# Two halves of the product with v, or one: where twelve matmuls of each head stand in TensorE's queue

## The chip, the cores and the metric

One core of a Trainium2 chip runs the whole program. The metric is device time in microseconds of one execution: 716.66 us before, the median of three runs (716.38 to 716.92). A NeuronCore has five engines, each with an instruction queue of its own that it works through in program order: TensorE (PE in the rows; its weight loads are PEld), VectorE (DVE), ScalarE (ACT), GpSimd (POOL) and SyncE (SP, which issues most DMAs here). They meet by semaphores. TensorE writes to PSUM; VectorE and ScalarE read it.

## The reference

Two layers, one after the other. First, attention over 2 batches x 8 heads of 768 positions and head size 64: q and k are each hashed to a bucket of 6 sign bits (the signs of q @ proj and k @ proj); a score counts only where the buckets agree, all others become -1e9; softmax over a row; product with v. Second, a mixture of 4 experts on the 1536 rows of 512 columns (the 8 heads side by side): for each expert, relu(x @ w1) @ w2, times the expert's normalized share, summed.

```python
mask = q_bucket[:, :, :, None] == k_bucket[:, :, None, :]
scores = np.where(mask, scale * np.matmul(q, k.transpose(0, 1, 3, 2)), -1000000000.0)
attn = np.exp(scores - np.max(scores, axis=-1, keepdims=True))
attn = attn / (np.sum(attn, axis=-1, keepdims=True) + 1e-09)
x = np.matmul(attn, v)                    # heads side by side: 1536 x 512
for e in range(E):
    out += p[:, e:e + 1] * (np.maximum(x @ w1[e], 0.0) @ w2[e])
```

## The kernel before

Everything is unrolled, and the order in the program is the order on each engine. First batch 0's attention runs alone (to about 131 us); then the experts for batch 0 run on TensorE with batch 1's attention interleaved; then the experts for batch 1.

Attention is written out as a software pipeline. A head has 768 query rows, six tiles of 128, and one tile is begun per step; `seq` lists the 96 tiles, step i begins tile i, and head x owns steps 6x to 6x+5 (called steps 0 to 5 of that head below). In each step, operations are issued in the order of the string `ORDER = "TXSUVMEYNRP"`, each for the tile or head that is due after its lag:

- **T** (`stage_t`, batch 0 only; lag 3): six 128x128 transposes on TensorE (L477) of a tile of exponentials into two PSUM banks (`ptps`), and two copies out of them, the first by ScalarE (L483), the second by VectorE (L481) in two of three steps and by ScalarE in the third. The copies go to `pt` (first three tiles of a head) or `pth` (last three).
- **S** (`stage_s`, lag 0): four matmuls (L409, L411) make the tile's scores in one of two PSUM buffers (`sps`); the hash bits are in the stacked operands, so that a wrong bucket falls away. VectorE copies them to `p` with a row reduction (L416), which frees the buffer.
- **U** (`stage_u`): when a head's product with v is finished, ScalarE (L560) copies its first half of rows out of PSUM and VectorE (L558) the second, into `xf`. `xf` holds a pair of heads (even and odd) and has one buffer per half.
- **V** (`stage_v`): the product with v. For each of six 128-row chunks of keys, two matmuls stand side by side in the array (`tile_position`), one per half of the head's query rows: twelve matmuls, each two records in the trace, accumulating in one PSUM bank `pv`. V is issued in parts.
- **M** (`stage_m`, lags 10 and 11, only after odd heads): GpSimd divides the pair by the row sums and splits it into two operands for the experts (L571, L573, L576), one half of the rows per step.
- **E** (`stage_e`, lag 1): ScalarE's exponential with the row sum (L432; an accumulator read follows it).
- **N**, **R**: reciprocal of the row sums on VectorE (L443, L444), and DMAs that turn and spread it.
- **P**: preparation of the next head. In step 1 ScalarE makes the high part `ah` (L338) and GpSimd copies it; in step 2 VectorE makes the low part `al` (L341); in step 3 four matmuls on TensorE make the hash (`hps`, L353), ScalarE takes its signs (`k`, L363), and GpSimd makes the bits (L368, L232); in step 5 VectorE turns the head after it (`xt`, L299). For the heads of batch 1 from the second on, the hash and high part stand in step 0.
- **X**, **Y**: batch 1's transposes by VectorE (L496) and DMA, in place of T.

Between steps, from the middle of batch 0, a generator adds the splits of the first expert's weights: VectorE's high parts (`w1hi`, `w2hi`, L705) and GpSimd's low parts (L698).

A lag counts from the head's last tile: lag 4 of a head is step 3 of the next head, lag 6 its step 5, lag 7 step 0 of the head after, lag 9 step 2. The banks `ptps`, `hps`, `pv` (and later the experts' `mps`) share four PSUM buffers. The lags of V are picked by batch, and U's lag follows from V's last one (`LAG_U` is 3 for batch 0); the last head of batch 0 has `LAST_V = (4, 5)`:

```python
def v_lags(b, h):
    return LAST_V if (b, h) == (0, H - 1) else LAG_V[not mixed(b, h)]
def u_lag(b, h):
    return v_lags(b, h)[-1] + (1 if (b, h) == (0, H - 1) else LAG_U[not mixed(b, h)])
```

`mixed` is true for the eight heads of batch 0.

Of the kernel before, what the change touches and what calls it, by code (L numbers as in the profile page):

```python
# [25 lines left out]
LAG_T = 3  # L26
LAG_X = 2
LAG_Y = 4
LAG_V = ((4, 6), (7,))
LAST_V = (4, 5)  # L30
LAG_U = (3, 1)
LAG_M = (10, 10)
# [19 lines left out]
def tile_lsh_attention__then__domain_moe(  # L52
# [345 lines left out]
    def mixed(b, h):  # L398
        return b * H + h < LIGHT_FROM
# [186 lines left out]
    def v_lags(b, h):  # L586
        return LAST_V if (b, h) == (0, H - 1) else LAG_V[not mixed(b, h)]

# [491 lines left out]
```

## Time and profile before

| | |
|---|---|
| median of three runs | 716.66 us |
| profiled execution | 716.44 us |
| its span | 714.7 us (the rest, 1.74 us, lies around it) |
| TensorE busy | 704.7 us, 99% of the span |
| VectorE / ScalarE / GpSimd busy | 482.1 / 293.3 / 302.6 us |
| granted TensorE clock | 1.00 |
| first batch's attention | from the start to about 131 us |

A busy share is an average over all stages: in the first 131 us VectorE and ScalarE have far more to do than later. Matmul records overlap (one begins while the one before drains), so what a group of matmuls costs is read from one group's start to the start of the next, not from its length. The same holds on ScalarE and VectorE, where the next instruction begins some 0.1 us before the last one's record ends. A bracket at the end of a row gives the idle time of that engine before the row, and what ended it.

### The profile page before, as it was taken

What the parts mean: (1) busy time and instruction counts of PE and PEld (TensorE: products, weight loads), DVE (VectorE), ACT (ScalarE), POOL (GpSimd) and SP (SyncE); (2) the same over time, 40 slices, a digit from 0 to 9 for tenths busy, and PEclk for the clock granted to TensorE, in tenths of its full rate; (3) what the DMA queues carried; (4) which work ended last, traced back from release to release, by engine and by line L of the source; (5) the groups of instructions that cost most, each with busy time, mean ns of one, the idle gap of its engine ahead of it and who ended that gap; (6) DMA issues with size and microseconds to landing.
All of it is one profiled execution on the core that took longest, in us unless ns stands there. A gap on an engine that the chain in (4) does not pass through costs nothing.

```text
span 714.7 us, 10131 instructions
## 1 busy us (share of the span) xinstructions
PE 704.7 (99%) x3750; PEld 597.3 (84%) x3750; DVE 482.1 (67%) x802; ACT 293.3 (41%) x580; POOL 302.6 (42%) x283
## 2 busy tenths in 40 slices
PE   8999999999999999999999999999999999999997
PEld 6766675787977979798888889898998989989896
DVE  6898898875756658575633234986858667685863
ACT  6887888442423324413120103443524434353340
POOL 6359578513255335240422244743424234342420
PEclk9999999999999999999999999999999999999999
DMA  6323344777867977777765112331122022121202
GB/s 148 65 49 76 73 98 92 210 180 191 249 155 209 239 209 188 214 207 240 231 203 137 59 46 74 89 119 59 60 89 88 30 89 59 60 79 69 89 1 88
DMA packets 90848, 87.76 MB, mean 123 GB/s; under 512 B 53168, under 2 KB 55728, under 8 KB 90800
## 3 DMA queue, kind: packets, MB, share of 16 engines
q1 hardware_dynamic: 89776, 86.80, 44.4%
q8 instruction: 29, 0.48, 0.3%
q10 hardware_dynamic: 1024, 0.33, 0.2%
q14 instruction: 19, 0.16, 0.1%
HBM read 65.04 MB, written 22.07 MB: 122 GB/s over the span
## 4 chain that ended last, share of the span: by engine, by line
PE 92%; DVE 3%; ACT 2%; POOL 1%; issue 1%; DMA 0%; POOLq 0%; DVEq 0%; ACTq 0%
PE mps L737 12%; PE mps L739 12%; PE mps L738 12%; PE pv L531 8%; PE mps L797 6%; PE mps L798 6%; PE mps L799 6%; PE sps L411 4%; PE sps L409 4%; PE ptps L477 4%; PE mps L952 2%; PE mps L948 2%; PE mps L951 2%; PE pd L948 2%; PE pa L952 2%; PE pa L951 2%
## 5 line engine op out<-in xcount | busy, mean ns | idle before, releaser
L737 PE MATMUL mps<-w2hi,hh 128*128 128x512 f32 (+1 forms) x388 | 151.1, 389 | 0.0
L739 PE MATMUL mps<-w2hi,hl 128*128 128x512 f32 (+1 forms) x388 | 150.7, 388 | 0.0
L738 PE MATMUL mps<-w2lo,hh 128*128 128x512 f32 (+1 forms) x388 | 150.5, 388 | 0.0
L731 DVE SCALAR_TENSOR_TENSOR acc<-mps,pe,acc 128x512 f32<-128x512 f32 (+1 forms) x85 | 63.0, 741 | 69.5 <-PE mps L739 69.0
L432 ACT ACTIVATE p<-p,nb 128x768 f32<-128x768 f32 x96 | 89.5, 932 | 34.7 <-DVE p L416 34.2
L416 DVE TENSOR_SCALAR_CACHE_REDUCE p<-sps 128x768 f32<-128x768 f32 x96 | 90.0, 939 | 18.8 <-PE sps L411 17.5
L803 ACT ACTIVATE hh<-mps 128x384 fp32r<-128x384 f32 x64 | 31.4, 491 | 170.0 <-PE mps L799 170.0
L934 POOL TENSOR_TENSOR w2lo<-ws,w2hi 128x512 fp32r<-128x512 f32 x32 | 40.6, 1288 | 108.4 <-ACT w2hi L933 108.4
L797 PE MATMUL mps<-xs,w1hi 128*128 128x384 f32 x256 | 86.3, 337 | 0.0
L798 PE MATMUL mps<-xs,w1hi 128*128 128x384 f32 x256 | 86.1, 336 | 0.1
L799 PE MATMUL mps<-xs,w1lo 128*128 128x384 f32 x256 | 86.0, 336 | 0.0
L739 PEld LDWEIGHTS mps<-w2hi,hl 128*128 128x128 f32 x388 | 72.9, 188 | 15.5
L737 PEld LDWEIGHTS mps<-w2hi,hh 128*128 128x128 f32 x388 | 72.9, 188 | 15.0 <-issue 1.2
L738 PEld LDWEIGHTS mps<-w2lo,hh 128*128 128x128 f32 x388 | 73.0, 188 | 14.1
L698 POOL TENSOR_TENSOR w1lo<-ws,w1hi 128x512 fp32r<-128x512 f32 x32 | 41.3, 1292 | 93.4 <-DVE w1hi L705 66.9
L804 DVE SCALAR_TENSOR_TENSOR hl<-mps,hh 128x384 fp32r<-128x384 f32 x64 | 35.6, 557 | 63.6 <-ACT hh L803 63.0
L531 PE MATMUL pv<-pt,tv 128*64 128x384 f32 x288 | 67.1, 492 | 0.0
L698 POOL TENSOR_TENSOR w2lo<-ws,w2hi 128x512 fp32r<-128x512 f32 x32 | 41.3, 1291 | 56.1 <-DVE w2hi L705 41.5
L409 PE MATMUL sps<-ah,q 128*128 128x384 f32 x192 | 53.9, 362 | 1.2 <-DVE p L416 1.2
L893 POOL TENSOR_TENSOR w1lo<-ws,w1hi 128x512 fp32r<-128x512 f32 x24 | 37.0, 1546 | 36.4 <-ACT w1hi L889 23.1
L531 PEld LDWEIGHTS pv<-pt,tv 128*64 128x64 f32 x288 | 24.9, 136 | 32.0 <-issue 31.1
L411 PE MATMUL sps<-k,al 76*128 76x384 f32 x192 | 49.9, 340 | 1.0 <-POOL k L232 0.6
(137 smaller groups left out, 1386.3 us busy)
## 6 DMA issues: line engine op xcount, KB each, us to landing
ws<-in_moe_w_dram SPq DMA_DIRECT2D x64, 512.0 KB, 4.0
scr<-t SPq DMA_DIRECT2D x16, 1152.0 KB, 8.2
pt<-scr SPq DMA_DIRECT2D x64, 288.0 KB, 5.9
tv<-in_v_dram SPq DMA_DIRECT2D x16, 192.0 KB, 5.0
tqk<-in_q_dram SPq DMA_DIRECT2D x30, 96.0 KB, 3.2
out_dram<-acc SPq DMA_DIRECT2D x11, 256.0 KB, 2.0
tqk<-in_k_dram SPq DMA_DIRECT2D x28, 96.0 KB, 3.5
rdb<-row SPq DMA_DIRECT2D x14, 192.0 KB, 5.1
```

Source lines behind the costliest of these rows:

```text
L409: nc.tensor.matmul(ps[:, i, :NH], q1[:, sl], k1[:, i * NH : (i + 1) * NH], start=True, stop=False)
L411: nc.tensor.matmul(ps[:, i, :NH], q2[0:MQE, sl], k2[0:MQE, i * NH : (i + 1) * NH], start=False, stop=True)
L416: nc.vector.tensor_scalar(out=two(pt), in0=ps[:, :, :NH], scalar1=MASKED, scalar2=MASKED, op0=ALU.min, op1=ALU.min, accum_out=nb,)
L432: nc.scalar.activation(pt, pt, ACTF.Exp, bias=nb, scale=-1.0, accum_out=dens[b, h, r][:, o : o + 1])
L531: nc.tensor.matmul(dst, vvs[b, h][:, c], pts[b, h, g][c], start=c == 0, stop=c == NT - 1, tile_position=(0, g * D),)
L698: nc.gpsimd.tensor_tensor(out=lo[:, c - 1], in0=st[c - 1], in1=hi[:, c - 1].bitcast(F32), op=ALU.subtract)
L737: nc.tensor.matmul(ps, hh[:, ts], w2hi[:, f, cs], start=n == 0, stop=False)
L738: nc.tensor.matmul(ps, hh[:, ts], w2lo[:, f, cs], start=False, stop=False)
L739: nc.tensor.matmul(ps, hl[:, ts], w2hi[:, f, cs], start=False, stop=n == FC - 1)
L797: nc.tensor.matmul(ps[:, :SB], w1hi[:, kk, fs], xhi[b, kk][:, sl], start=kk == 0, stop=False)
L798: nc.tensor.matmul(ps[:, :SB], w1hi[:, kk, fs], xlo[b, kk][:, sl], start=False, stop=False)
L799: nc.tensor.matmul(ps[:, :SB], w1lo[:, kk, fs], xhi[b, kk][:, sl], start=False, stop=kk == KD - 1)
```

## The change

One constant. For heads 0 to 6 of batch 0, V is issued in one part at lag 4 (step 3 of the next head) and no more in two halves at lags 4 and 6 (steps 3 and 5). As `stage_v` divides the six chunks by the number of parts, the one part has all twelve matmuls. As U's lag is counted from V's last, U of these heads moves from lag 9 to lag 7. Head 7 (`LAST_V`) and batch 1 (second entry) are as before.

```diff
-LAG_V = ((4, 6), (7,))
+LAG_V = ((4,), (7,))
```

## Rows read from the trace of the kernel before

**Rows 1.** The page: busy time by engine, and VectorE's costliest attention line.
```profile
PE 704.7 (99%) x3750; PEld 597.3 (84%) x3750; DVE 482.1 (67%) x802; ACT 293.3 (41%) x580; POOL 302.6 (42%) x283
...
L416 DVE TENSOR_SCALAR_CACHE_REDUCE p<-sps 128x768 f32<-128x768 f32 x96 | 90.0, 939 | 18.8 <-PE sps L411 17.5
```

**Rows 2.** Busy time by stretch: start:end, length, engines, clock, DMA share, GB/s.
```profile
24.03:37.60 13.57, 13.57 (x90) 9.53 (x89) 10.64 (x21) 11.35 (x25) 6.00 (x8) 1.00 0.36 63
37.60:51.24 13.64, 13.64 (x90) 9.51 (x89) 12.11 (x27) 11.21 (x25) 6.56 (x9) 1.00 0.33 60
51.24:65.81 14.57, 13.87 (x89) 9.51 (x88) 11.74 (x24) 11.57 (x25) 12.83 (x14) 1.00 0.14 39
65.81:79.40 13.59, 13.59 (x90) 9.54 (x89) 11.11 (x22) 11.23 (x25) 7.27 (x9) 1.00 0.68 154
79.40:93.15 13.75, 13.72 (x89) 9.51 (x88) 12.47 (x24) 11.66 (x25) 12.01 (x13) 1.00 0.10 28
93.15:107.68 14.53, 13.55 (x89) 9.57 (x88) 13.41 (x25) 11.13 (x25) 9.36 (x11) 1.00 0.53 102
107.68:122.05 14.37, 14.17 (x87) 8.91 (x86) 12.01 (x23) 12.27 (x26) 12.47 (x14) 1.00 0.38 73
```

**Rows 3.** Timeline of TensorE over one head: start us, us, instruction.
```profile
37.60 0.54 PE L531 MATMUL pv<-pt,tv 128*64 128x384 f32 x1
...
37.97 0.48 PE L531 MATMUL pv<-pt,tv 128*64 128x384 f32 x1
...
39.58 0.82 PE L353 MATMUL hps<-xt,pf 128*44 128x384 f32 x4
40.33 0.87 PE L477 MATMUL ptps<-ident,p 128*128 128x128 f32 x6
...
41.74 1.05 PE L477 MATMUL ptps<-ident,p 128*128 128x128 f32 x6
...
43.42 0.54 PE L531 MATMUL pv<-pt,tv 128*64 128x384 f32 x1
...
45.51 0.88 PE L477 MATMUL ptps<-ident,p 128*128 128x128 f32 x6
```

**Rows 4.** Timeline of ScalarE over the same head.
```profile
40.51 1.16 ACT L363 ACTIVATE k<-hps,sgn_bias 44x384 fp32r<-44x384 f32 x2 [1.13 <-PE hps L353]
...
42.59 0.94 ACT L432 ACTIVATE p<-p,nb 128x768 f32<-128x768 f32 x1
...
43.90 0.92 ACT L432 ACTIVATE p<-p,nb 128x768 f32<-128x768 f32 x1
...
46.10 0.49 ACT L483 ACTIVATE pth<-ptps 128x384 f32<-128x384 f32 x1 [1.18 <-PE ptps L477]
...
47.45 0.87 ACT L483 ACTIVATE pth<-ptps 128x384 f32<-128x384 f32 x2
48.21 0.94 ACT L432 ACTIVATE p<-p,nb 128x768 f32<-128x768 f32 x1
```

**Rows 5.** Timeline of all engines in a step before the first V.
```profile
15.47 0.94 ACT L432 ACTIVATE p<-p,nb 128x768 f32<-128x768 f32 x1
...
16.55 0.33 PE L477 MATMUL ptps<-ident,p 128*128 128x128 f32 x1 [0.71 <-ACT p L432]
```

**Rows 6.** Timeline of all engines: M's last operations, and U of head 2.
```profile
62.97 1.01 POOL L576 TENSOR_TENSOR xs<-xf,xs 128x384 fp32r<-128x384 f32 x1
...
65.51 0.56 DVE L558 COPY xf<-pv 64x384 f32<-64x384 f32 x1
...
91.03 1.02 POOL L576 TENSOR_TENSOR xs<-xf,xs 128x384 fp32r<-128x384 f32 x1
```

**Rows 7.** Timeline of all engines at the change from batch 0 to batch 1.
```profile
115.35 0.98 DVE L299 STREAM_TRANSPOSE xt<-tqk 128x768 f32<-128x768 f32 x1
...
117.09 0.53 PE L353 MATMUL hps<-xt,pf 128*44 128x384 f32 x2
...
120.36 1.14 DVE L341 SCALAR_TENSOR_TENSOR al<-xt,qk_scale,ah 128x768 fp32r<-128x768 f32 x1
```

## The prediction

> **What bounds the kernel now.** I read the page's busy times first, then busy time by stretch over the first batch, then the timelines of TensorE, ScalarE, VectorE and GpSimd around one head, then what each waits for. The reader should see that TensorE is busy for 704.7 of 714.7 us [rows 1], and that the first batch is a strict rhythm: from one head's V to the next takes 13.57 to 14.57 us [rows 2]. TensorE's busy time fills these stretches to within a hair in four of them and lacks 0.70 and 0.98 us in two, so TensorE's instruction stream sets the pace. But ScalarE is busy for 11.13 to 12.27 us and VectorE for 10.64 to 13.41 us of each [rows 2], both in program order with little room. The granted clock is 1.00 in all of them.
>
> One head's rhythm on TensorE [rows 3]: first part of V at 37.60, hash matmuls (in P) at 39.58, step 4's T and S from 40.33, step 5's from 41.74, second part of V at 43.42, and the next step's T at 45.51. A step without V thus costs 1.41 us, the first part 1.98 and the second 2.09. ScalarE [rows 4] waits exactly twice in this head, each time behind a part of V: 1.13 us for the hash (before the sign at 40.51) and 1.18 us for the transposes after the second part (46.10). Between the two it runs almost without a gap: exponentials start at 42.59 and 43.90, and after 46.10 it runs on through the copies at 47.45 and the exponential at 48.21.
>
> **The change part by part.** *Moved: the second part of V, seven times.* Heads 0 to 6 have LAG_V's first entry; head 7 has LAST_V, batch 1 the second entry. The same 12 matmuls (24 records) are issued; the second six come two steps earlier, between the first six and the hash. Merged they take 1.98 + 6 pairs x 0.32 (39.58 less 37.97, over five) = 3.90 us against 1.98 + 2.09 = 4.07. So 0.17 us a head is saved on TensorE itself, 1.2 us in all [rows 3]. The switches between tile shapes cost this. The Trainium skill (TensorEngine Tiling (Array Packing), Tiling Modes, Key Properties) says that changing the tiling mode drains TensorE; the trace agrees with its 0.17 us, and by that alone the change would be faster (first rival).
>
> *What loses its cover.* Set zero at the start of step 4's T (40.33). On ScalarE the sign starts at +0.18, then come step 4's two copies, the exponential E of step 3's scores at +2.26 and, after one copy, the next at +3.57 [rows 4]. All that follows the hash, so none of it moves against it. T needs an exponential three steps old in scores: in step 0 of the next head T wants the one begun at +2.26. How soon can it follow? An E began at 15.47 and the T that waited for it went at 16.55 [rows 5]: 1.08 us, its accumulator read included. Before, T of step 0 came at 45.51 = +5.18 and E had long ended. Now it could start at +3.09, where V's second part stood, and must wait to 2.26 + 1.08 = 3.34. Going on: ScalarE's copy for step 0 follows E at 3.57 + 0.93 = 4.50. Then U, which the change also moves (below), is taken at 0.37, like a copy of the same width (43.90 less 42.59 less 0.93). The next E starts at 5.24; two copies (48.21 less 47.45, 0.76) and its own 0.93 later the next, at 6.93. TensorE: T of step 1 at 3.34 + 1.41 = 4.75 (its E: 3.57 + 1.08 = 4.65, in time); T of step 2 at 6.32 (E 5.24 + 1.08; TensorE ready at 6.16); T of step 3 at 8.01 (6.93 + 1.08; ready at 7.73). V follows 1.44 later, at 9.45. With 3.90 for V and 0.75 for the hash (40.33 less 39.58) the period is 14.10 us, where a TensorE that waited for nobody would need at most 13.64 - 0.17 = 13.47. The same read from ScalarE: its 11.1 to 11.3 us of work stays, its two waits of 1.13 and 1.18 become one of about 2.9, because after the last E of a head nothing in its queue can run before the sign, and the sign stands behind the whole of V. V's time is what ScalarE and VectorE used to catch up in; split, both halves were used, merged, half is wasted.
>
> *Moved: U, from lag 9 to lag 7.* u_lag is the last lag of V plus 3, so U of heads 0 to 6 comes two steps earlier too, in step 0 where it stood in step 2. No DMA is issued by V or U, so SP's queue is as before, and M (lags 10, 11, on GpSimd) stays. ScalarE's and VectorE's copies (0.37 and 0.48 us from start to start) only change places; the PSUM bank of pv comes free two steps sooner. T of step 3 ran 0.14 us longer than others before, by the timeline for want of a bank, so this is worth between 0 and 0.14 us a head; I take 0, as T of steps 2 and 3 now waits for E anyway.
>
> *A wait that this adds.* The buffer xf has one copy; U of an even head writes it after M of the odd head before has read it. For head 2 M's last GpSimd operation began at 62.97 and took 1.01, and VectorE's U began at 65.51 [rows 6]: 1.5 us of room, and U is moved up by two steps, some 2.8 us. M's place is fixed to V by the chain VectorE al, GpSimd ah, w1lo, M, al, k, M: its end was 63.98 - 51.24 = 12.74 after V; with U out of step 2 al starts about 0.1 us sooner, so 12.64, which is +7.99 after step 4's T (V and hash take 4.65). VectorE would be ready for U at +6.4 to +6.9. VectorE's U takes 0.48 from start to start. Queued behind it: the reduction of step 1's scores (0.94 to 0.95 us [rows 1]), which releases the score buffer that S of step 3 needs (two buffers). So U 8.04 to 8.52, reduction to 9.47, S of step 3 at 9.52 and not at 8.59, V at 10.39: the period from V of head 2 to V of head 3 is 15.04. Likewise at head 4: M ended at 92.05, 12.65 after V at 79.40, less 0.2; U 7.85, reduction to 9.28, period 14.85. At head 6 M (its chain ends 11.3 after V) is early enough. Bounds of this wait: 0, if GpSimd runs ahead, and 1.6 us (7.99 less 6.4) a time.
>
> *The sum, interval by interval against [rows 2].* Head 0 to 1: 14.10 - 13.57 = +0.53. 1 to 2: 14.10 - 13.64 = +0.46. 2 to 3: 15.04 - 14.57 = +0.47; the 0.70 us that TensorE lost there (14.57 less 13.87, nearly all for GpSimd's k by the waits) stays but now runs while ScalarE catches up. 3 to 4: 14.10 - 13.59 = +0.51. 4 to 5: 14.85 - 13.75 = +1.10. 5 to 6: the old loss of 0.98 us (T behind a VectorE copy that stood behind w2hi) goes, as that T now comes 2 us later; but a row's reciprocal and the turn of the next head on VectorE make the reduction of step 0 end near 7.5, so 14.67 - 14.53 = +0.14. After head 6's V: in step 0 of batch 1's first head a second hash (117.09) needs the turned tile xt, made from 115.35 to 116.33 [rows 7]. V's second part stood before it as cover; now TensorE waits there some 1.2 us (xt ready at +5.9, TensorE at +4.7). VectorE's al (120.36, +9.95) comes at about +9.15, zero comes 1.92 later after V than before, and U's 0.48 has gone from VectorE's chain behind it, which ends the batch: 1.92 - 0.80 - 0.48 = +0.64. Sum: +3.85 us. From there TensorE is full, so the delay passes to the end. The profiled execution took 716.44, so 720.3; the median of the runs is 0.22 higher, so 720.5.
>
> **The rivals.** *Faster: TensorE alone decides.* If the exponentials turn out to be ready (ScalarE 82% busy, so it could be), only the switches count: 7 x 0.17 = 1.2 us, with the sooner free PSUM bank up to 7 x 0.31 = 2.2: 714.5 to 715.5. The point from which it decides is E's 1.08 us: T of step 0 must find its E done by +3.09, 0.25 us sooner than I have it, and T of step 3 by 7.6. For it: TensorE's full stretches [rows 2]; against it: ScalarE's gapless runs [rows 4] and T's wait in the steps before the first V [rows 5]. The rule of the Trainium skill to look at the most-contended engine by occupancy (Perfetto Trace Analysis, Identifying the Most-Contended Engine) stands on this side: TensorE's work only shrinks. 10%.
>
> *No change.* ScalarE's waits come out at half my size and the xf wait at zero: 5 x 0.25 + 0.3 - 1.2, so 717.0. 17%.
>
> *Only ScalarE's hole, no wait on xf.* Then head 2 to 3 is 14.10 (-0.47), 4 to 5 is 14.10 (+0.35): 3.85 - 0.94 - 0.75 = +2.2, 718.8. 20%.
>
> *VectorE becomes the bound in each head.* It has 12.1 to 13.4 us of work in three intervals; if each costs the 1.10 of head 4 to 5: 6 x 1.1 + 0.64 = +7.2, 723.9. Against it: its own hole behind V swallows al and the weight casts. 8%.
>
> **How the numbers follow.** The forecast has 45%. Slower by over 0.2% (1.4 us, about what can be told from no change here) are it, the hole alone and the last rival, 0.73 less 0.01 for the hole's lower edge: 0.72; within 0.2%: 0.18; faster: 0.10. The range from 716.8 to 722.5 leaves out the faster rival, half of no change and the last.
>
> **What would show it.** Right: 24 records of V in a row for 3.90 us; ScalarE waiting about 2.9 us before the sign and no more 1.18 after V; T of steps 0, 2 and 3 put down to E; VectorE's U of heads 2 and 4 waiting for GpSimd's last M; the hash of batch 1's first head waiting for xt; intervals near 14.1. Wrong: intervals near 13.4, T not waiting for E, or a first batch that ends on time while the loss comes later.

## The result, and the profile after

The changed kernel takes 722.68 us (median of four runs, 722.4 to 723.07) against 716.79 before (four runs): +5.9 us, a ratio of 1.0086 with a 95% interval of 1.0073 to 1.0098. Slower was forecast, at 720.5 with 722.5 as the range's upper end; the measured time lies 0.2 us above that end.

The page after: busy time by engine, and the line that answers to the second of [rows 1].

```profile
PE 706.7 (98%) x3750; PEld 599.3 (83%) x3750; DVE 479.8 (67%) x802; ACT 292.6 (41%) x580; POOL 303.3 (42%) x283
...
L416 DVE TENSOR_SCALAR_CACHE_REDUCE p<-sps 128x768 f32<-128x768 f32 x96 | 89.9, 938 | 30.8 <-PE sps L411 30.1
```

No engine has more instructions than before [rows 1]: VectorE's 802 take 2.3 us less of busy time, TensorE's 3750 are busy for 2.0 us more. What has grown is VectorE's idle time ahead of its reductions, 18.8 to 30.8 us, put down to scores from TensorE that come late.

Busy time by stretch, from one head's V to the next, answering to [rows 2] (same columns):

```profile
24.79:38.87 14.08, 13.82 (x90) 9.47 (x89) 10.83 (x22) 11.09 (x25) 5.61 (x7) 1.00 0.33 60
38.87:53.28 14.41, 13.88 (x89) 9.46 (x88) 11.86 (x27) 11.30 (x25) 7.16 (x9) 1.00 0.28 57
53.28:68.55 15.27, 14.08 (x89) 9.58 (x88) 11.59 (x24) 11.59 (x26) 14.41 (x16) 1.00 0.18 54
68.55:83.03 14.48, 13.63 (x89) 9.58 (x88) 11.80 (x25) 11.10 (x25) 6.28 (x7) 1.00 0.57 127
83.03:98.92 15.89, 13.93 (x90) 9.55 (x89) 11.52 (x22) 11.46 (x26) 14.89 (x17) 1.00 0.20 42
98.92:113.45 14.53, 13.89 (x90) 9.53 (x89) 11.41 (x25) 11.10 (x25) 6.36 (x7) 1.00 0.42 77
113.45:128.73 15.28, 13.75 (x87) 9.05 (x86) 11.36 (x24) 12.10 (x27) 12.87 (x15) 1.00 0.42 71
```

Every stretch is longer than before except the sixth, and TensorE no longer fills any of them: its busy time lacks 0.26 to 1.96 us in each. Against the sum of the prediction:

| from V of head to V of head | before | forecast | after | change forecast | change measured |
|---|---|---|---|---|---|
| 0 to 1 | 13.57 | 14.10 | 14.08 | +0.53 | +0.51 |
| 1 to 2 | 13.64 | 14.10 | 14.41 | +0.46 | +0.77 |
| 2 to 3 | 14.57 | 15.04 | 15.27 | +0.47 | +0.70 |
| 3 to 4 | 13.59 | 14.10 | 14.48 | +0.51 | +0.89 |
| 4 to 5 | 13.75 | 14.85 | 15.89 | +1.10 | +2.14 |
| 5 to 6 | 14.53 | 14.67 | 14.53 | +0.14 | 0.00 |
| 6 to the end of the batch | 24.54 | 25.18 | 25.33 | +0.64 | +0.79 |
| sum | | | | +3.85 | +5.80 |

(The last line before the sum runs from V of head 6 to the hash matmuls in step 0 of batch 1's second head, at 132.22 before and 138.78 after.) The 5.80 us account for the measured 5.9. The two profiled executions lie further apart, 723.07 and 716.44, but 0.76 us of that stood there already at the first V, ahead of which the change does nothing; across the profiles of this study in which the hash stands behind V, that first V came between 23.95 and 24.79 us.

TensorE over one head, answering to [rows 3] (hash and everything after it 3.21 us later by the clock, as V of head 1 began 1.27 later and lasts 1.94 longer):

```profile
42.79 0.81 PE L353 MATMUL hps<-xt,pf 128*44 128x384 f32 x4
43.54 0.87 PE L477 MATMUL ptps<-ident,p 128*128 128x128 f32 x6
...
44.95 1.04 PE L477 MATMUL ptps<-ident,p 128*128 128x128 f32 x6
...
46.88 0.87 PE L477 MATMUL ptps<-ident,p 128*128 128x128 f32 x6 [0.18 <-ACT p L432]
...
50.11 0.92 PE L477 MATMUL ptps<-ident,p 128*128 128x128 f32 x6 [0.30 <-ACT p L432]
```

ScalarE over the same head, answering to [rows 4]:

```profile
43.71 1.16 ACT L363 ACTIVATE k<-hps,sgn_bias 44x384 fp32r<-44x384 f32 x2 [2.99 <-PE hps L353]
...
45.80 0.94 ACT L432 ACTIVATE p<-p,nb 128x768 f32<-128x768 f32 x1
...
47.10 0.93 ACT L432 ACTIVATE p<-p,nb 128x768 f32<-128x768 f32 x1
...
48.02 0.48 ACT L483 ACTIVATE pth<-ptps 128x384 f32<-128x384 f32 x1
48.52 0.48 ACT L560 ACTIVATE xf<-pv 64x384 f32<-64x384 f32 x1
49.03 0.94 ACT L432 ACTIVATE p<-p,nb 128x768 f32<-128x768 f32 x1
```

V lasts 3.92 us (38.87 to 42.79; 3.90 forecast). ScalarE's two waits have become one of 2.99 us before the sign (2.9 forecast). With zero at step 4's T (43.54), the exponentials begin at +2.26 and +3.56, as forecast, and T of step 0 follows at +3.34, to the hundredth. T of step 2 comes 1.08 us after the exponential at 49.03, also as forecast; but that exponential began at +5.49 and not at +5.24. A bracket marks the transposes for which TensorE stood waiting; the kernel before had none in this head.

### The profile page after: what moved, and what is told of

Same layout as the page of the kernel before. It is cut to its first block, busy times and chain, and to the rows that moved or that the text cites. A ratio compares the mean times of both kernels' runs of the same rounds, so it can differ in the third digit from the quotient of the medians.

```text
span 721.3 us, 10131 instructions
## 1 busy us (share of the span) xinstructions
PE 706.7 (98%) x3750; PEld 599.3 (83%) x3750; DVE 479.8 (67%) x802; ACT 292.6 (41%) x580; POOL 303.3 (42%) x283
## 4 chain that ended last, share of the span: by engine, by line
PE 88%; POOL 3%; ACT 3%; DVE 2%; issue 2%; DMA 1%; ACTq 0%; POOLq 0%
PE mps L737 12%; PE mps L739 12%; PE mps L738 12%; PE pv L531 7%; PE mps L797 6%; PE mps L798 6%; PE mps L799 6%; PE sps L409 3%; PE sps L411 3%; PE mps L952 2%; PE mps L948 2%; PE mps L951 2%; ACT p L432 2%; PE pd L948 2%; PE pa L952 2%
## 5 line engine op out<-in xcount | busy, mean ns | idle before, releaser
L416 DVE TENSOR_SCALAR_CACHE_REDUCE p<-sps 128x768 f32<-128x768 f32 x96 | 89.9, 938 | 30.8 <-PE sps L411 30.1
L531 PE MATMUL pv<-pt,tv 128*64 128x384 f32 x288 | 65.6, 490 | 0.0
```

Source lines behind the costliest of these rows:

```text
L416: nc.vector.tensor_scalar(out=two(pt), in0=ps[:, :, :NH], scalar1=MASKED, scalar2=MASKED, op0=ALU.min, op1=ALU.min, accum_out=nb,)
L531: nc.tensor.matmul(dst, vvs[b, h][:, c], pts[b, h, g][c], start=c == 0, stop=c == NT - 1, tile_position=(0, g * D),)
```

## The experiments

Eleven kernels beside the change, each compared with the kernel before on the same chip in five rounds. Theory A is the prediction's: V ahead of the hash leaves ScalarE without work, and U's move adds work in step 0 and a wait on xf. The clean intervals below are those from head 0 to 1, 1 to 2 and 3 to 4: no M stands in them, nor the waits that the kernel before already had between heads 2 and 3 and between 5 and 6. In kernels with added lines the line numbers of `kernel.py` are up to 14 higher than those above.

**The merge without U's move.**

```diff
-LAG_U = (3, 1)
+LAG_U = (5, 1)
```

> V merged as in the change, but U left at lag 9 (LAG_U 5 for batch 0). Theory A (V ahead of the hash starves ScalarE; U's move then adds ScalarE work in step 0 and a wait on xf at heads 2 and 4): the hole before the sign stays near 2.9 us, but without U in step 0 the exponential of step 1 comes 0.4 to 0.6 us sooner; period 13.8 to 13.9 us, no VectorE wait for GpSimd's M, in all +1 to +2 us over the kernel before, 717.8 to 718.8. Rival B (the loss is U's move alone): the loss of 5.9 us goes wholly, 716.8 or less. Rival C (the merge alone): 722.7 as with the change.

Measured: 718.21 us, ratio 1.0024 (1.0014 to 1.0034), +1.7 us. The three clean intervals are 13.71, 13.96 and 13.85, and ScalarE's wait before the sign is 2.3 to 3.0 us. VectorE's U never waits for M: its one wait that is put down to GpSimd, 0.57 us at head 4, comes 1.4 us after M's end and names the weight split behind M. So of the 5.9 us the merge alone causes 1.7, and 0.75 of these lie at the turn of the batch (25.29 us there for 24.54). Rivals B and C both fall.

**U's move without the merge.**

```diff
-LAG_V = ((4,), (7,))
-LAG_U = (3, 1)
+LAG_V = ((4, 6), (7,))
+LAG_U = (1, 1)
```

> V in two parts as before, but U moved to lag 7 (LAG_U 1 for batch 0): the second half of the change alone. Theory A: intervals without an M stay at 13.5 to 13.7; VectorE waits for GpSimd's M at heads 2 and 4 by some 2 us each, which costs 0.5 us between heads 2 and 3 and 2 us between heads 4 and 5: +1.5 to +2.6 in all, 718.3 to 719.4. Rival B (U's move alone): 722.7. Rival C (the merge alone): 716.8.

Measured: 718.35 us, ratio 1.0035 (1.0023 to 1.0048), +1.9 us. The timeline of VectorE at head 4's U:

```profile
92.91 0.56 DVE L558 COPY xf<-pv 64x384 f32<-64x384 f32 x1 [2.01 <-POOL xs L576]
93.39 1.00 DVE L705 CAST w2hi<-ws 128x512 fp32r<-128x512 f32 x1
94.42 0.96 DVE L416 TENSOR_SCALAR_CACHE_REDUCE p<-sps 128x768 f32<-128x768 f32 x1
```

VectorE waits 2.01 us for GpSimd's M here and 1.33 at head 2, where some 2 us each were expected (and 0.82 at head 6, which was not). The intervals 2 to 3 and 4 to 5 are 15.28 and 15.94, about as long as in the change (15.27, 15.89): these two are set by M and by what stands behind U on VectorE, however V stands. The parts do not add: 1.7 and 1.9 make 3.6 of 5.9. The other 2.3 us come of having both. Counted by interval, 1.1 us of them lie in the clean ones and 1.5 between heads 5 and 6 and at the turn of the batch, where U's move alone had gained 0.81 and 0.62 us and the change keeps neither; the two intervals with M give back 0.4. That V's second part in step 5 had covered what U brings into step 0 is how theory A reads this; no run tests it.

**The wait on xf taken away.** A second buffer for the half that VectorE writes, so that U writes while M still reads the other:

```diff
-                    xf[b, j, g] = xs.tile([P, GN], F32, tag=f"xf{g}", name="xf", bufs=1)
+                    xf[b, j, g] = xs.tile([P, GN], F32, tag=f"xf{g}", name="xf", bufs=1 + g)
```

> The change, with two buffers for the half of xf that VectorE writes, so that U of heads 2 and 4 has no reader to wait for. Theory A: VectorE's waits for GpSimd's M (2.7 us in the trace after) go; between heads 2 and 3 14.4 instead of 15.27, between 4 and 5 about 14.6 instead of 15.89; 720.6, that is 2.1 less than the change. If the wait on xf is hidden by ScalarE's lateness: 722.5.

Measured: 720.34 us, ratio 1.0055 (1.0043 to 1.0068), +3.9 us where the change has +5.9; between heads 2 and 3 14.43 us, between 4 and 5 14.75. The wait on xf is on the path, and no other single edit here gives back as much of the loss without undoing half of the change.

**The hash ahead of V, nothing else.** The four matmuls of `hps` become a function of their own, called before V's first part; the sign and all that follows stay in P (the function itself is left out here):

```diff
+                            if lag == 4 and bh != (0, H - 1) and part == 0 and bh[0] == 0:
+                                hash_of(*hseq[hseq.index(bh) + 2])
                             stage_v(*bh, part, len(v_lags(*bh)))
```

> The change, with only the four hash matmuls of a head moved from behind V to ahead of it on TensorE; the sign and all other work stand where they stood on their queues. Theory A (the hole on ScalarE comes from the sign standing behind V): the sign runs during V, the exponential of step 3 comes 0.9 us sooner after V, T of steps 0, 2 and 3 no longer waits; 13.5 to 13.7 us in the three intervals without a wait on xf and 14.0 between heads 5 and 6, the two with that wait as with the change; 719.7. If the hole comes from V's length alone, whatever stands behind it: 722.5.

Measured: 723.28 us, ratio 1.0092 (1.0078 to 1.0105), no better than the change: the expected 719.7 failed, but not for the reason under test. From hash to hash the clean intervals are 13.48, 13.81 and 13.74, as theory A had them (14.08, 14.41 and 14.48 in the change). ScalarE's timeline in this kernel:

```profile
39.44 1.17 ACT L373 ACTIVATE k<-hps,sgn_bias 44x384 fp32r<-44x384 f32 x2
42.79 0.87 ACT L493 ACTIVATE pt<-ptps 128x384 f32<-128x384 f32 x2 [2.18 <-PE ptps L487]
43.68 0.94 ACT L442 ACTIVATE p<-p,nb 128x768 f32<-128x768 f32 x1
```

The sign runs during V, and the first exponential behind V comes 1.48 us after T's start (42.20) and no more 2.26 after it. The 1.9 us gained in the clean intervals were lost again further on: 0.87 in the interval from head 4 to 5, with the second of the waits on xf, which grew to 16.76 us, 0.56 in the next (15.09), and 1.56 at the turn of the batch (26.89 for 25.33). TensorE in the first of these:

```profile
94.01 0.55 PE L487 MATMUL ptps<-ident,p 128*128 128x128 f32 x3 [1.03 <-DVE xf L568]
95.92 0.73 PE L419 MATMUL sps<-ah,q 128*128 128x384 f32 x2 [1.37 <-DVE p L426]
96.45 0.84 PE L421 MATMUL sps<-k,al 76*128 76x384 f32 x2
```

M ends 12.2 us after V began, where it ended after 12.4 in the change, so a TensorE that gets there sooner waits longer; and after the two gaps the granted clock falls. The windows of this kernel show 0.57 from 95.90 to 98.50:

```profile
95.90:98.50 2.60, 2.58 (x8) 1.32 (x10) 2.57 (x7) 2.37 (x5) 1.40 (x2) 0.57 0.68 107
```

At the turn of the batch the same happens: the hash in step 0 of batch 1's first head waits 1.97 us for the turned tile, and the clock is 0.76 from 120 to 127. So one cause was taken away, and the two waits behind it, with the lower clock that followed them, took its time; how much of the loss is the clock's alone no run separates.

**Both causes away, the merge kept.** The hash ahead of V, and U at lag 9.

> V merged, the hash matmuls ahead of it as in e4, and U left at lag 9 as in e1: both costs of the change taken away at once, the merge itself kept. Theory A: 13.4 to 13.6 us between heads 0, 1, 2 and between 3 and 4; 14.6 between 2 and 3 (GpSimd's k stays), 13.6 to 14.0 between 4, 5 and 6, 15.0 to 15.3 between 6 and 7, where no second part of V covers the hash that waits for xt: 716.3, within 0.6. If a merged V costs something of its own: 718.2 as in e1.

Measured: 717.03 us, ratio 1.0009 (1.0001 to 1.0018), +0.7 us, 0.1 above the expected span. The clean intervals: 13.48, 13.75, 13.48; between 4, 5 and 6 14.13 and 14.15, more than expected; from head 6's hash to head 7's V 14.75, less than expected. A merged V costs next to nothing once the sign doesn't stand behind it and U stays: against e1, which differs only in the place of the hash, 1.7 us have become 0.7.

**The same with head 6 split as before.**

```diff
+        if (b, h) == (0, H - 2):
+            return (4, 6)
         return LAST_V if (b, h) == (0, H - 1) else LAG_V[not mixed(b, h)]
```

A like line, left out here, keeps U of head 6 at lag 9.

> As e5, but head 6 keeps V in two parts (lags 4 and 6). Theory A, with the loss at the turn of the batch put down to V's second part of head 6 having been the cover of the hash of batch 1's first head: 14.3 to 14.5 between heads 6 and 7, 0.7 less than e5: 715.6. If the turn of the batch costs for another reason: as e5.

Measured: 716.59 us, ratio 1.0003 (0.9994 to 1.0012). From head 6's hash to the end of the batch it is 24.87 us instead of 25.29 in e5, so the split of head 6 gives 0.4 us and not 0.7; the expected 715.6 was 1 us too low.

**The change with head 6 split**, the edit just shown on the changed kernel; U of head 6 falls at lag 9 again by it.

> The change for heads 0 to 5 only; head 6 keeps V in two parts and U at lag 9. Theory A: between heads 6 and 7 14.4 to 14.6 instead of 15.28, but U of head 6 is back on VectorE's last chain of the batch (0.5 us): 722.0 to 722.2, half a microsecond less than the change. If head 6 has no part in the loss: 722.6.

Measured: 721.47 us, ratio 1.0072 (1.0059 to 1.0086). From V of head 6 to the end of the batch 24.47 us against 25.33 in the change and 24.54 before. So the 0.8 us of the table at the turn of the batch are head 6's part of the change, and they go wholly, where 0.5 was expected; as e1 has them too, with U in its old place, they are the merge's and not U's.

**The cast behind U moved.** One weight split called one step later:

```diff
-            if i > W_SPLIT and i % W_STEP == 0:
+            if i > W_SPLIT and (i in W_MOVED.values() or (i % W_STEP == 0 and i not in W_MOVED)):
```

with `W_MOVED = {96: 98}`. The numbers count the pieces in which the attention program is handed out, two or three to a step; with VectorE's cast goes a low part on GpSimd.

> The change, with one of the weight splits (VectorE's w2hi that stood between U of head 4 and the reduction behind it, and GpSimd's low part issued with it) called one step later, after that reduction. Theory A (my sum missed 1.04 us between heads 4 and 5 because that cast stands behind the waiting U and ahead of the reduction, so that the wait hides nothing of it): 14.85 instead of 15.89 us there, 721.6 in all. If the cast is hidden, or its place makes no difference: 722.6.

Measured: 721.58 us, ratio 1.0071 (1.0058 to 1.0083); between heads 4 and 5 14.96 instead of 15.89. VectorE still waits 1.40 us at U there, and the reduction follows U at once:

```profile
94.83 0.56 DVE L559 COPY xf<-pv 64x384 f32<-64x384 f32 x1 [1.40 <-POOL xs L577]
95.42 0.96 DVE L417 TENSOR_SCALAR_CACHE_REDUCE p<-sps 128x768 f32<-128x768 f32 x1
```

**The kernel before, with the hash ahead of V's first part.**

> The kernel before, with the four hash matmuls moved ahead of the first part of V. Theory A: ScalarE's 1.13 us before the sign shrinks, but TensorE sets the pace there, so only the 0.1 to 0.2 us a head go that T of step 5 waits for the bank of the hash: 715.3 to 716.5. If ScalarE's wait for the hash were on the path before already: 714 or less.

Measured: 715.70 us, ratio 0.9993 (0.9984 to 1.0001): not to be told from no change by its interval, though in the trace the three clean intervals are 13.39 each (13.57, 13.64 and 13.59 before).

**And the splits that stood in the way.** On e8, `W_MOVED = {102: 104}`, the w2hi between al and the copy for T:

> The kernel before with the hash ahead of V (e8) and one weight split, the one that stood between VectorE's al and its copy for T after head 5's V, called one step later. T no longer waits 0.98 us for that copy: 13.4 to 13.6 instead of 14.5 us between heads 5 and 6, 714.7. If the time is only given back at the turn of the batch, where VectorE's chain is the longest: 715.7.

Measured: 714.92 us, ratio 0.9977 (0.9968 to 0.9986); between heads 5 and 6 13.55 instead of 14.53. Then `W_MOVED = {54: 58, 102: 104}`, which also takes w1lo from ahead of M and k on GpSimd:

> As e10, and the weight split whose low part stood on GpSimd ahead of M and of k between heads 2 and 3 called four yields later, behind them. S of head 4's first tile no longer waits 0.65 us for k: 13.9 instead of 14.6 us between heads 2 and 3, 714.1. If GpSimd's M alone makes k late: as e10.

Measured: 713.93 us, ratio 0.9964 (0.9951 to 0.9976). GpSimd's timeline in this kernel:

```profile
56.26 1.01 POOL L587 TENSOR_TENSOR xs<-xf,xs 128x384 fp32r<-128x384 f32 x1
57.37 0.95 POOL L379 TENSOR_SCALAR al<-k,bit_mul 44x768 fp32r<-44x768 f32 x1
58.41 0.83 POOL L233 TENSOR_SCALAR k<-al 12x768 fp32r<-12x768 f32 x1
59.32 1.29 POOL L712 TENSOR_TENSOR w1lo<-ws,w1hi 128x512 fp32r<-128x512 f32 x1
```

k is done before the low part begins, and the interval 2 to 3 is 13.38, where 13.9 was expected. This kernel, with V split, is faster than both: by 2.6 us than the one before, which is itself 5.9 faster than the change.

## Why the prediction was right or wrong

*Right: the direction, and why.* The sign behind the whole of V, ScalarE's one long wait, T of step 0 following an exponential by 1.08 us (in all six intervals; T of step 2 in three of them): the trace shows each at its place. That the hash's place behind V makes them is shown by e4, in which all three clean intervals fall below 13.9 with the hash ahead, and in the whole time by e5 against e1. The first interval came at 14.08 for 14.10.

*Right: the added wait.* VectorE's U waits for M 1.34 and 1.41 us at heads 2 and 4 in the changed kernel, 2.7 us in all; e3 takes it away and gains 2.0. e2 and e1 show that it belongs to U's move alone. Between 2 and 3 the interval is 0.23 above the forecast: M ended 12.73 us after V and not 12.64, U took 0.59 and not 0.48.

*Wrong: the size.* The sum was 3.85 and is 5.80, and two terms make most of the difference. The larger is the step "U 7.85, reduction to 9.28, period 14.85" at head 4. It lets the reduction follow U, but on VectorE's queue a weight cast stands between the two. VectorE's timeline in the changed kernel:

```profile
95.47 0.56 DVE L558 COPY xf<-pv 64x384 f32<-64x384 f32 x1 [1.41 <-POOL xs L576]
95.95 1.02 DVE L705 CAST w2hi<-ws 128x512 fp32r<-128x512 f32 x1
97.00 0.96 DVE L416 TENSOR_SCALAR_CACHE_REDUCE p<-sps 128x768 f32<-128x768 f32 x1
```

and TensorE's:

```profile
98.03 0.61 PE L409 MATMUL sps<-ah,q 128*128 128x384 f32 x2 [1.37 <-DVE p L416]
```

In the kernel before, VectorE's rows were these:

```profile
89.81 0.77 DVE L705 CAST w2hi<-ws 128x512 fp32r<-128x512 f32 x1
90.50 0.95 DVE L416 TENSOR_SCALAR_CACHE_REDUCE p<-sps 128x768 f32<-128x768 f32 x1
...
93.07 0.56 DVE L558 COPY xf<-pv 64x384 f32<-64x384 f32 x1 [0.27 <-issue]
```

Here too the cast ran just ahead of a reduction, but U came 3 us after it; the prediction moved U and left the cast where the clock had it, ahead of U, instead of where the queue has it, behind U. That term was 1.10 and measured 2.14; e9 moves the cast and gets 14.96 us for the forecast 14.85. Of what is queued behind the waiting U the prediction counted the reduction only.

The other is that U "is taken at 0.37, like a copy of the same width". That holds for even heads, as head 4 shows:

```profile
92.18 0.47 ACT L483 ACTIVATE pth<-ptps 128x384 f32<-128x384 f32 x1
92.55 0.47 ACT L560 ACTIVATE xf<-pv 64x384 f32<-64x384 f32 x1
92.92 0.94 ACT L432 ACTIVATE p<-p,nb 128x768 f32<-128x768 f32 x1
```

For an odd head, whose rows go to the upper 64 partitions, ScalarE starts U only when the copy before has ended and the exponential only when U has: in the rows of head 1 in the section on the result, 48.02 to 49.03 for copy and U, 1.01 us where head 4 takes 92.18 to 92.92, 0.74. These 0.27 us make the exponential of step 1 late (+5.49 for +5.24) and with it T of step 2 in the interval 1 to 2 (+0.31 over the forecast). In the interval 3 to 4 (+0.38) they are only a part: the exponential began 0.19 us late there, and T followed it by 1.46 us and not by 1.08, a wait put down to ScalarE's copy behind that exponential; why T waited for that copy there stays open. That the odd heads cost this is read from the rows; no run changed it. The trace of before had it: U of odd heads stood between gaps there too (50.46 to 50.97).

*The turn of the batch* was forecast at +0.64 and is +0.79; the hash waits for xt as forecast, and e7 shows that head 6's split is what covers it:

```profile
123.26 0.98 DVE L299 STREAM_TRANSPOSE xt<-tqk 128x768 f32<-128x768 f32 x1
...
124.38 0.85 PE L353 MATMUL hps<-xt,pf 128*44 128x384 f32 x4 [1.35 <-ACT p L432]
```

The profile puts this wait down to an exponential of ScalarE, but the hash begins 0.14 us after xt's end (124.24), as it does within 0.01 us in e1, e4 and e5, where the same wait is put down to xt. *Heads 5 to 6* came out at 0.00 for +0.14: the reduction of step 0 ended at +7.2 and not near 7.5, and T's waits there (0.19, 0.29 and 0.15 us) are put down to exponentials alone.

*The rivals.* TensorE alone (715), no change (717.0) and ScalarE's hole alone (718.8) are refuted by the table: the saving is there, 1.98 + 2.09 - 3.92 = 0.15 us a head for 0.17 forecast, but it doesn't decide. That a change of tiling mode drains TensorE, as the Trainium skill has it (TensorEngine Tiling (Array Packing), Tiling Modes, Key Properties), is in keeping with these 0.15 us; no run separates the drain from anything else that a second start of V costs. The rule of the Trainium skill to look at the most-contended engine by occupancy (Perfetto Trace Analysis, Identifying the Most-Contended Engine) did not tell the direction here. For TensorE that section of the Trainium skill judges headroom by the share of peak reached and the busy share of the weight loads, and not by that of the matmuls. By the weight loads (84% before) as by the matmuls (99%) TensorE came first [rows 1]; the change took 0.15 us a head from it, and the time rose. VectorE as the bound in each head (723.9) came near in time, but its mechanism is not there: in four of six intervals TensorE has no wait that is put down to VectorE. The range ended at 722.5 because the forecast's own terms were given no spread upwards: only the xf wait had an upper bound, and the bound did not hold the work queued behind it.

## What to carry to other kernels

A block of matmuls that is long for TensorE is the time in which the engines that feed it catch up; what stands behind it in program order decides whether they can. Before one is merged, look for the small producer behind it (here four hash matmuls) whose consumer heads another engine's queue, and issue that first. And an operation that is moved up on a queue is to be placed by the queue's order, with every instruction that is then behind it, not by the times at which its neighbours ran before.

## What the runs showed of the hardware that had not been expected

ScalarE's copy out of PSUM of 64 x 384 took 0.48 us in either half of the partitions, but its neighbours overlapped with it (0.37 from start to start) only where it wrote the lower 64 partitions; where it wrote the upper ones it stood alone (0.51 to the next instruction, and 0.50 after the one before). In batch 1 of the kernel before, lower copies too began 0.38 and 0.39 us after a copy ahead of them (368.04 and 238.75) and upper ones 0.51 and 0.52 (336.30 and 270.86), but there the exponential behind a lower copy came only after 0.50 us (238.75 to 239.25), so the half alone does not decide. Why is open: whether the partitions or a semaphore wait does it was not tried.

In e4 TensorE stood idle for 1.03 us before 94.01 and for 1.37 before 95.92, and then ran at a granted clock of 0.57 from 95.90 to 98.50, near the lower of its two levels of 1.2 and 2.4 GHz, with matmul records of 0.84 for 0.52 us. In the changed kernel the one wait of 1.37 us before 98.03 was not followed by that: the stretches on both sides show 1.00.
